# Block products with nested sums, four chained in one PSUM bank, and redrawn instruction lists for tiles 3 to 8

## The chip, the core and the metric

One NeuronCore of a Trainium2 chip runs the whole program. The metric is device time in microseconds; the runs of the kernel before gave 348.14, 348.18 and 349.24 us, a median of 348.18. Engines are named as the profile names them: PE (matrix products), PEld (its weight loads), DVE, ACT and POOL (element-wise work), SP (it only issues DMAs). POOL also issues DMAs.

## The reference

Causal attention in blocks of 64 over 8 batches, 8 heads, 576 positions and head width 64; its output, laid out as 4608 tokens by 512, goes through a gated feed-forward layer.

```python
def _attn_ref(q, k, v):
    scores = 1.0 / np.sqrt(D) * np.matmul(q, k.transpose(0, 1, 3, 2))
    scores = np.where(block_i >= block_j, scores, -1000000000.0)
    attn = np.exp(scores - np.max(scores, axis=-1, keepdims=True))
    attn = attn / (np.sum(attn, axis=-1, keepdims=True) + 1e-09)
    return np.matmul(attn, v)

def _moe_ref(x, w_gate, w_val, w_out):       # x: 4608 x 512
    gate = np.maximum(x @ w_gate, 0.0)       # 512 x 1536
    val = x @ w_val
    return gate * val @ w_out                # 1536 x 512
```

## The kernel before

**Tiles.** The feed-forward work is cut into nine tiles of 512 tokens: tile j (0 to 7) is the first 512 positions of batch j, and tile 8 collects the last 64 positions of all eight batches. Hidden values are kept transposed, in three buffers hT of four chunks (128 hidden units by 512 tokens). While tile j is in the feed-forward layer, the attention of batch j+1 is computed between its matmuls, so that tile 7 and tile 8 have no attention work beside them.

**Who sets the order.** All instructions are issued in an order written out by hand; each engine works through its own instructions in that order and waits on semaphores. Tiles 0 to 2 come from a generator of matmuls into which the other work is put at given places. Tiles 3 to 6 share one list, `ORDER_3_6`; tiles 7 and 8 have their own. A list holds tokens: `p15*2` is two steps of product 5 of pair 1 (one step is two matmuls of 128 x 256), `p1a` an element-wise step of pair 1, `g0` and `v0` one plain matmul of 128 x 512, `M4` two matmuls of out-product 4, `oa` a step of the out-projection, `A1` the score matmuls of visit 1 (one visit for two heads), `E1u` one of its exponentials, `C11` a zeroing of masked corners, `V10` the product with v of one head, `N10` its normalisation, `T2` a DMA transpose of normalised outputs on SP's queue, `l0` to `l10` the loads of q and k of the batch after next and `w0` to `w5` those of v (POOL's queue), `d0` to `d3` their DMA transposes (SP's queue), `K` the scores of the last 64 positions, `X` a sum of parts of the tile's input x, `s` a sum of parts of the hidden values, `U` a sum of weights that is made once, `S` a store.

**Seven products.** In tiles 3 to 8 the up-projection of a pair of hidden chunks (gate and value) is done as a 2 x 2 block product with seven products in place of eight. `times` (line 1331) issues one: two steps of two matmuls, left operand a weight block or a sum of weight blocks (`up_sum`, line 922), right operand a block of x or a sum of blocks (`x_sums`, line 1130). Tiles 3 to 6 take four pairs (1, 2, 3, 5) so and four chunks plainly; tiles 7 and 8 take all six pairs so. The seven products of a pair go into three PSUM tiles:

- y takes products 5, 3, 6, z takes 2, 4, 7, and m takes 1;
- ACT copies y after product 5 (`a`, line 1371) and z after product 2 (`b`, line 1374), and z again after product 4 (`l`, line 1389); a ReLU of y after product 3 gives the gate of the second half (`r`);
- DVE or POOL adds the two copies (`s`, line 1377), DVE subtracts that sum from m (`m`, line 1382), adds y (`y`, line 1393) and z (`z`, line 1396);
- the halves of the hidden pair are then `H` (a product, on POOL or DVE, line 1401) and `L` (a product with the ReLU in the same instruction, DVE, line 1415).

The out-projection (`seven_products`, line 1011) does the same with hidden sums (`Sums.make_part`, line 976, the add at line 992; 18 DVE instructions per tile) and sums of rows of w_out: products 3 and 5 in one bank, 4 and 2 in another, 1, 6 and 7 in three more; three ACT copies (`oa`, `oy`, `oz`) and six adds (line 1080).

PSUM has eight banks here: two tiles `sc` of two banks each, one tile `one`, three tiles `ffnp`. A visit needs both `sc` tiles, `one` and an `ffnp` at a time; `PAIR_BANK` says which tile takes y, z and m of each pair.

Of the kernel before, what the change touches and what calls it, by code (L numbers as in the profile page):

```python
# [17 lines left out]
def kernel(  # L18
# [23 lines left out]
    OUT_2 = (3, "oa", 4, "ob", 1, "om", 5, "oy", 2, "oz", "S0", "oc", "od", 6, "o6", "S1", 7, "o7", "S2")  # L42
# [3 lines left out]
            "010101010101010010101010101010101010101010101010101010101001110010100110"  # L46
            "100111001010011010011100101001101001110010100110100110100101"
# [3 lines left out]
            "201021102101020120120120121201202101202101202101210210201102220201101202"  # L51
            "001201202112000202112102022102102011022202011012020012012021120002021121"
            "0202210210122001201200121012012"
        ),
        "ob": (
            "043210432104310420312142324014203124304232410421302431423240142031243042"
            "324104210324103140231403"
        ),
        "gate_sb": (
            "021021021021021021021021021021021021021021011201201002102101120120100210"  # L60
            "21021021"
        ),
    }
    ORDER_3_6 = """
        A0 E0t X1 X3 X4 X6 Y4 g0 X7 E0u E0s C01 E0f g0 K g0*2 r0 k g1*2 v0*2 C00 l0 l1
        l2 v0 p15 v0 h0 p15 p1a g1*2 V00 U02 N00 r1 P V01 N01 p12*2 p1b p1s p13 l3 w0
# [4 lines left out]
        p36*2 p3y r8 p34*2 p3l V11 N11 A2 E2t E2u E2f p2L p37*2 p3z U41 w2 w3 p52*2  # L71
        s1101 p55*2 s0212 p3L p5b v8*2 V10 N10 p51 v8*2 h8 p5a p53*2 p51 p54 p5s p5m E2s
        C21 g9*2 p54 s1201 p5r p56 g9 p56 g9 p5l p57 r9 p57 v9*4 p5y p5z C20 h9 M3*2 A3
        E3t p5L s2001 E3s p3H U45 s1012 s2101 s1112 s1001 E3u p5H s2112 U05 E3f U07
        s2012 V21 N21 C31 M4 M3*2 M4 M3*2 U46 U47 w4 w5 C30 V20 N20 M1*3 M4*3 T1 T0 oa
# [4 lines left out]
        p15 p05 X1 p05 p0a p02*2 p0b p12*2 p1b p01 X3 X4 p03 p0s p03 p0r p15 p1a p04*2  # L80
        p0l p01 p1s X6 p06*2 p13*2 p1r p25*2 X7 p07*2 p0m p0y p0H Y1 p0z p0L p11 p22*2
        p11 P p2a p2b p2s p23*2 p2r p16 p14*2 p1l p16 p1m p1y p24 p26 p21*2 p26 s0101
        p24 p2l p1H p35*2 p3a p2m p2y p32*2 p27*2 p45 p3b p3s p45 p4a s0001 p2H p2z
        p17*2 p1z p33 p34 p33 p55 p42*2 p3r p34 p31*2 p2L p4b p4s p1L p3l p36*2 p55 p5a
        p3m p3y p3H s1101 p43*2 p4r p44 p37*2 p3z p3L s0112 p52 p41 p46 p52 p5b p41 p4m
        p53*2 p5r p5s p51 p44 p4l p51 p46 p4y p54 p47 p56 p54 p4H p5m p56 p5y p5l M4 p47
        p4z p57*2 p5z M3 M4 M3 M1 p5H M4*4 p4L p5L s1012 s1112 M3 s2112 s2101 M3*3 oa
        s0012 s1001 M1*5 M5 s2001 M5 s2012 M5*4 oy S0 ob M2*5 s0212 s0201 M6 s1201 s2212
        M2 M7 s1212 M6 s2201 oz S1 M6 M7 M6*3 om oc od o6 Y3 M7*4 o7 S2
    """  # L90
    ORDER_8 = """
        X6 p12*2 p1b p15*2 p1a p1s X7 p02*2 p0b p05*2 p14 p11*2 p13*2 p0a p0s p1m p01
        p03 p14 p01 p0m p03 p1r p16*2 p1y p1H p1l p17*2 p1z p0r p06*2 p04*2 P p0y p22*2
        p1L p0l p0H p2b s0112 p25*2 p32*2 p35 p07 p35 p2a p2s p07 p0z p0L p23*2 p3a p24
        p21*2 p2m p24 p2r p26*2 p3b p3s p2y p2H p55 p2l p33*2 p31 p34 p31 p34 p3r p36
        s0001 p3m p36 p3y p3H p55 p27*2 s0101 p2z p3l p37*2 p3z p52*2 p51 p5a p42 p45*2
        p5b p54 p53*2 p2L p3L p5s p42 s1001 p41 p4a p43 p41 p51 p43 p5r p56 p5m p56 p54
        p5y p4b p4s p44*2 p4m p5H p4r M3 p46*2 p5l p57 p4l p47*2 p57 M3 p4y p4z p5z M4*2
        p4H M4*3 p4L p5L M1 M4 M3*3 s1012 s1101 s2101 M3 s1112 M1 s2112 M1*3 oa s0012 M5
        s2001 M5 s2012 M5*4 ob oy S0 s2212 M2*5 M1 s0212 s2201 M2 oz S1 s1212 s0201  # L100
        s1201 M6*6 om oc o6 M7*6 S2 od o7b Sb o7a Sa
    """
    ONLY = {
        'U01': (6,),
        'U02': (6,),
# [3 lines left out]
        'U41': (6,),  # L109
        'U42': (6,),  # L110
# [3 lines left out]
        'Y4': (6,),  # L114
# [10 lines left out]
        (3, 1): ('sc', 'ffn', 'sc'),  # L125
        (3, 2): ('one', 'sc', 'ffn'),
        (3, 3): ('sc', 'ffn', 'ffn'),
        (3, 5): ('ffn', 'one', 'sc'),
        (4, 1): ('sc', 'ffn', 'sc'),
        (4, 2): ('one', 'sc', 'ffn'),  # L130
        (4, 3): ('sc', 'ffn', 'ffn'),
        (4, 5): ('ffn', 'one', 'sc'),
        (5, 1): ('sc', 'ffn', 'sc'),
        (5, 2): ('one', 'sc', 'ffn'),
        (5, 3): ('sc', 'ffn', 'ffn'),
        (5, 5): ('ffn', 'one', 'sc'),
# [33 lines left out]
    AV_BANK = {0: ('sc', 'one'), 1: ('ffn', 'ffn'), 2: ('sc', 'ffn'), 3: ('ffn', 'sc')}  # L170
    U_AT = {'U15': 300, 'U12': 306, 'U11': 312, 'U16': 386, 'U17': 389, 'U25': 320, 'U22': 326, 'U21': 332, 'U26': 392, 'U27': 395, 'U35': 340, 'U32': 346, 'U31': 352, 'U36': 398, 'U37': 401, 'U55': 360, 'U52': 366, 'U51': 372, 'U56': 404, 'U57': 407}
# [738 lines left out]

    def weight_differences(c, eng):

        two = wo[c // 2][:, 2 * (c % 2) : 2 * (c % 2) + 2, :]
        for d, n in ((two[:, 0, 256:512], two[:, 1, 256:512]), (two[:, 1, 0:256], two[:, 0, 0:256])):
            eng.tensor_tensor(out=d, in0=d, in1=n, op=AX.subtract)
# [6 lines left out]
    def up_sum(n, which):  # L922
# [6 lines left out]
        g, u = wg[i], wv[i]  # L929
        a, b, op = {  # L930
            1: (g[:, 0:2, f], u[:, 2:4, f], AX.add),
            2: (u[:, 0:2, f], u[:, 2:4, f], AX.add),
            5: (g[:, 0:2, f], g[:, 2:4, f], AX.add),
            6: (u[:, 0:2, f], g[:, 0:2, f], AX.subtract),
            7: (g[:, 2:4, f], u[:, 2:4, f], AX.subtract),
        }[which]
        if which in (6, 7):
            t = a
        else:
            where, i, k = UP_MEM[n][(5, 2, 1).index(which)]  # L940
# [11 lines left out]
    class Sums:  # L952
# [16 lines left out]
        def make(self, q, parts, k0, k1):  # L969
            while len(self.two) <= q:  # L970
                self.two.append(sb.tile([128, 2048], BF, name="stage", bufs=10))
            for part in parts:
                if part < 3:
                    self.make_part(q, part, k0, k1)
# [1100 lines left out]
```

## Time and profile before

| what | value |
|---|---|
| median of three runs | 348.18 us (348.14 to 349.24) |
| the profiled execution: its own time / its span | 348.39 us / 346.6 us |
| granted TensorE clock | 0.999 |
| instructions | 9051; 3481 matmuls recorded |
| busy PE / PEld / DVE / ACT / POOL | 334.8 / 233.9 / 273.0 / 207.5 / 194.7 us |
| read from and written to HBM | 37.75 MB and 9.44 MB |
| tile 3, 4, 5, 6 begins (score matmuls of visit 0) | 139.3, 175.3, 211.5, 247.4 us |
| tile 7, tile 8 begins (first matmul of a product) | 283.28, 312.31 us |
| last matmul ends / last DVE instruction ends | 341.72 / 342.73 us |

A busy share of an engine is the time that its instructions take in the records. Matmuls overlap: one of 128 x 256 has a duration of 273 ns, but 24 of them in a row take 2.78 us, which is (2.78 - 0.27) / 23 = 0.109 us from one start to the next, and four of 128 x 512 take 1.03 us, (1.03 - 0.38) / 3 = 0.217 us. What PE could still give away is therefore seen in the distances between starts and not in its busy share. A group of instructions names its line, its engine, the tile written and the tiles read, its count and its mean duration; the releaser behind a gap is what ended the wait.

### The profile page before, as it was taken

How to read it: one execution, taken by the hardware profiler on the slowest of the kernel's cores; microseconds unless marked ns; L12 is line 12 of the kernel's file. 1: busy time of each engine (PE TensorE's matmuls, PEld its weight loads, DVE VectorE, ACT ScalarE, POOL GpSimd, SP SyncE). 2: the span in 40 equal slices, each digit the busy share in tenths (PEclk: the TensorE clock that was granted, in tenths of full speed). 3: DMA queues.
4: the chain of work that ended last, by engine and by line, in shares of the span. 5: the costliest groups of instructions: out<-in, count | busy, mean ns of one | idle time of the engine just before them, and what ended most of it. 6: DMA issues, size and time to landing. Idle time of an engine off the chain costs nothing.

```text
span 346.6 us, 9051 instructions
## 1 busy us (share of the span) xinstructions
PE 334.8 (97%) x3481; PEld 233.9 (67%) x3518; DVE 273.0 (79%) x690; ACT 207.5 (60%) x341; POOL 194.7 (56%) x229
## 2 busy tenths in 40 slices
PE   8999999999999999999999999999999999999994
PEld 4544455545545559676977787778778788888873
DVE  4854455768629897789977997899899989999995
ACT  4942756587335872687468746884588537526721
POOL 2767566477795901986087627872155636612530
PEclk9999999999999999999999999999999999999999
DMA  8999999999999994999299929993400141012005
GB/s 244 294 352 373 360 217 242 229 155 176 184 218 113 137 191 82 190 174 139 40 158 181 152 40 156 164 171 47 121 32 2 33 129 33 2 41 83 3 0 121
DMA packets 155403, 50.07 MB, mean 144 GB/s; under 512 B 134464, under 2 KB 151744, under 8 KB 155360
## 3 DMA queue, kind: packets, MB, share of 16 engines
q1 hardware_dynamic: 77520, 32.52, 43.7%
q0 software_dynamic: 70528, 8.98, 43.3%
q10 hardware_dynamic: 7312, 8.00, 8.3%
q8 instruction: 27, 0.44, 0.5%
q14 instruction: 16, 0.13, 0.1%
HBM read 37.75 MB, written 9.44 MB: 136 GB/s over the span
## 4 chain that ended last, share of the span: by engine, by line
PE 75%; DMA 10%; DVE 9%; issue 2%; ACT 2%; POOL 1%; DVEq 0%; SPq 0%; ACTq 0%; POOLq 0%
PE ffnp L1033 11%; PE ffnp L1162 11%; PE ffnp L1348 9%; PE ffnp L1322 7%; PE sc L1348 7%; PE ffnp L1265 5%; PE one L1348 5%; PE one L1033 4%; PE sc L611 3%; DMA stage<-in_moe_w_out_dram 3%; PE ffnp L759 3%; DMA stage<-in_moe_w_val_dram 2%; DMA stage<-in_moe_w_gate_dram 2%; PE one L611 2%; DVE ob L1382 2%
## 5 line engine op out<-in xcount | busy, mean ns | idle before, releaser
L616 ACT ACTIVATE attnT<-sc 128x1024 bf16<-128x1024 f32 x56 | 56.3, 1037 | 0.0
L1033 PEld LDWEIGHTS <-stage 128*128 128x128 bf16 x420 | 39.9, 98 | 4.8 <-DVE stage L992 0.2
L992 DVE TENSOR_TENSOR stage<-hT 128x512 bf16<-128x512 bf16 (+2 forms) x120 | 39.6, 382 | 0.2
L1162 PE MATMUL ffnp<-xT,wg 128*128 128x512 bf16 x130 | 36.2, 379 | 0.6
L1172 ACT ACTIVATE gate_sb<-ffnp 128x512 bf16<-128x512 f32 x35 | 20.5, 598 | 27.0 <-PE ffnp L1162 22.7
L1080 POOL TENSOR_TENSOR ob<-ob,ob 128x512 f32<-128x512 f32 x7 | 8.9, 1268 | 45.7 <-DVE ob L1080 19.9
L1348 PEld LDWEIGHTS <-stage 128*128 128x128 bf16 x288 | 27.6, 98 | 7.4 <-issue 0.4
L759 PEld LDWEIGHTS <-attnT 128*128 128x128 bf16 x640 | 26.1, 98 | 9.2 <-DVE attnT L1526 1.1
L1033 PE MATMUL ffnp<-stage 128*128 128x256 bf16 x252 | 32.0, 273 | 0.0
L1162 PE MATMUL ffnp<-xT,wv 128*128 128x512 bf16 x108 | 31.3, 380 | 0.2
L1182 DVE TENSOR_TENSOR hT<-gate_sb,ffnp 128x512 bf16<-128x512 bf16 x28 | 19.1, 684 | 14.1 <-PE ffnp L1162 11.5
L623 ACT ACTIVATE attnT<-one 128x512 bf16<-128x512 f32 (+1 forms) x28 | 15.0, 536 | 22.2 <-PE ffnp L611 11.6
L489 POOL DMA_DIRECT2D v_bf<-in_v_dram x30 | 24.5, 826 | 3.5 <-PE sc L759 1.6
L1348 PEld LDWEIGHTS <-wg 128*128 128x128 bf16 x224 | 21.5, 98 | 5.7 <-issue 1.5
L1348 PEld LDWEIGHTS <-wv 128*128 128x128 bf16 x224 | 21.8, 98 | 4.1 <-DVE perm L1154 0.2
L1265 PE MATMUL ffnp<-wo,hT 128*128 128x512 bf16 x91 | 23.2, 379 | 0.3
L1162 PEld LDWEIGHTS <-wv 128*128 128x128 bf16 x144 | 12.9, 98 | 14.7 <-issue 1.8
L1162 PEld LDWEIGHTS <-wg 128*128 128x128 bf16 x144 | 13.4, 98 | 13.8 <-issue 0.5
L1401 POOL TENSOR_TENSOR hT<-gate_sb,ob 128x512 bf16<-128x512 bf16 x16 | 19.0, 1188 | 4.0 <-DVE ob L1393 3.9
L489 POOL DMA_DIRECT2D q_bf<-in_q_dram x20 | 18.0, 906 | 3.7 <-DVE recip L732 3.5
L611 PEld LDWEIGHTS <-kTm 64*128 64x128 bf16 x384 | 11.3, 94 | 12.9 <-issue 7.3
L1377 POOL TENSOR_TENSOR ob<-ob,ob 128x512 f32<-128x512 f32 x8 | 10.1, 1265 | 16.7 <-ACT ob L1371 10.2
(228 smaller groups left out, 911.7 us busy)
## 6 DMA issues: line engine op xcount, KB each, us to landing
out_dram<-ob ACTq DMA_DIRECT2D x28, 256.0 KB, 3.6
stage<-in_moe_w_val_dram SPq DMA_DIRECT2D x6, 512.0 KB, 8.7
stage<-in_moe_w_gate_dram SPq DMA_DIRECT2D x6, 512.0 KB, 8.3
stage<-in_moe_w_out_dram SPq DMA_DIRECT2D x6, 512.0 KB, 10.5
q_bf<-in_q_dram POOLq DMA_DIRECT2D x20, 128.0 KB, 4.8
k_bf<-in_k_dram POOLq DMA_DIRECT2D x20, 128.0 KB, 5.9
v_bf<-in_v_dram POOLq DMA_DIRECT2D x20, 128.0 KB, 6.3
stage<-in_v_dram SPq DMA_DIRECT2D x19, 128.0 KB, 5.4
```

What stands on the lines that cost most here:

```text
L489: ins = nc.gpsimd.dma_start(dst, part_of)
L611: nc.tensor.matmul(o, kTm[b % 2][head_of(hh), c, hp, :], qT, start=True, stop=True)
L616: return lambda: nc.scalar.activation(at[:, :, lo : lo + 512], sc, AF.Exp, scale=scale)
L759: nc.tensor.matmul(av[:, p, :], at[:, col : col + 128], v_bf[b % 2][:, c, h, :], start=(p == 0), stop=(c == p), skip_group_check=True,)
L992: nc.vector.tensor_tensor(out=out.rearrange("p (c n) -> p c n", c=m), in0=a, in1=b, op=op)
L1033: nc.tensor.matmul(to, sums.of(c)[which][:, 128 * p : 128 * p + 128], right, start=first, stop=(c == 5), skip_group_check=True,)
L1162: nc.tensor.matmul(to, (wg, wv)[t][f // 4][:, c, 128 * (f % 4) : 128 * (f % 4) + 128], x[:, c], start=(c == 0), stop=(c == 3),)
L1172: nc.scalar.activation(gate_sb, gate, AF.Relu)
L1182: nc.vector.tensor_tensor(out=h, in0=gate_sb, in1=val, op=AX.mult)
L1265: nc.tensor.matmul(op, hT[f][:, 128 * s : 128 * (s + 1)], wo[f // 4][:, f % 4, n0:n1], start=(f == 0), stop=(f == 11),)
L1322: nc.tensor.matmul(to, (wg, wv)[t][f // 4][:, c, 128 * (f % 4) : 128 * (f % 4) + 128], x[:, c], start=(c == 0), stop=(c == 3),)
L1348: nc.tensor.matmul(st[key][:, 256 * k : 256 * k + 256], left[:, c, 128 * k : 128 * k + 128], right[:, c], start=new and (k, c) == (0, 0), ...
```

## The change

It puts another scheme of seven products in place of the first, with sums that use each other, in both projections of tiles 3 to 8 and in the out-projection of tile 2; the same number of matmuls of the same sizes is issued (3518, 796,608 columns in all). The products of a pair now go so: the tile w takes products 1, 6, 5, 3 one after the other, v takes 7 and 4, and x takes 2. ACT copies w after product 1 (`a`) and after 6 (`u`) and v after 7 (`w`); DVE adds w after product 5 onto the copy of v (`d`), v after 4 onto the second copy (`e`) and x onto the first (`c`); `r` is the ReLU of w after product 3. `H` and `L` are as before.

- Sums of x: four in place of five, nested (5, then 6 from it, then 4 from that, and 7), three on POOL in tiles 3 to 7. Hidden sums: four parts of 512 columns for each hT buffer, 12 in place of 18 instructions, nested in the same way, five of them on POOL in tiles 3 to 7 and three in tile 8. Weight sums of the up-projection: four per pair in place of five, one written in place in wv, none in wg. Corners: five of eight on POOL.
- Out-projection: w takes products 1, 6, 5, 3 in one bank with reads `oa`, `ou` (ACT), `od` (DVE) between them and `oy` (ACT) last; v takes 7 and 4 (`ow` ACT, `oe` DVE); x takes 2 (`oc` DVE). Four ACT copies and three DVE adds.
- New lists: `ORDER_3_6`, `ORDER_7`, `ORDER_8`, `OUT_2`, `PAIR_BANK`, `OUT_BANK`, `SLOTS`, `ON_POOL`, `AV_BANK`. In `ORDER_3_6` the last loads of k (`l8`; `l9`, `l10`) and their transposes (`d1`, `d2`; `d3`) go from the first half of the list to its second half and its end. The places of the work in tiles 0 to 2 are written as a list (`ORDER_0`); up to the out-projection of tile 2 PE's instructions are the same as before.

The diff, cut:

```diff
     ORDER_3_6 = """
-        A0 E0t X1 X3 X4 X6 Y4 g0 X7 E0u E0s C01 E0f g0 K g0*2 r0 k g1*2 v0*2 C00 l0 l1
...
-        p13 p1r p11 v1*2 p11 l4 l5 p1m p14 p16*2 p1y d0 p14 p1l v1 U01 U06 U42 l6 l7 l8
-        d1 d2 A1 E1u v1 h1 p17*2 p32 E1t E1s E1f p25*2 p32 g8 p1z p1L C11 p22*2 g8*2
-        p35*2 C10 s0101 p1H s0112 p2a p23*2 p2b p24 p21 g8 p21 p24 p3b p2r p26 s0012 l9
-        l10 d3 w1 p3a p3s s0001 p26 p2s p2m p2y p2H p33*2 p31*2 p3m p2l p27*2 p2z p3r
...
-        M5 M1*2 M4 ob V31 M5 V30 M5 N31 M5*2 T2 N30 T3 M1 M5 M2*4 oy M2*2 S0 oz s0201
-        s2212 s1212 S1 s2201 M6*2 om M7 M6*3 oc od M7 M6 M7*4 o6 S2 o7
+        A0 E0u X5 X7 g0 g1*3 X6 X4 g0 p12*2 p11*2 g1 g0*2 E0f E0s p1a p1c p17*2 p16 w0
+        E0t C01 r0 K k p16 p1u C00 V00 N00 U05 l0 v1*2 p15*2 p1w p1d V01 N01 l1 l2 l3 r1
+        v0 p14*2 p1e p13*2 v0 p1L P p1r w1 l4 l5 A1 E1t E1u E1s v1*2 h1 p21 p22 p21 v0
...
+        V10 p5w p5u p54*2 p5e g9*4 p55*2 d0 E2f C20 l8 w5 N10 T1 r9 A3 E3u T0 d1 d2 v9*3
+        p5L s0102 M1 v9 p5d p53*2 E3s h9 s1102 M1*3 C21 p5r p5H E3f C30 M1 V21 s1002
+        s2102 s1202 s2002 M1 E3t V20 N21 N20 s0302 M7*2 T2 M7*3 oa M6 M7 ow C31 V31 N31
+        s2202 V30 M6 N30 M6 M4*2 M6*3 M4 U47 s2302 ou M4*3 U43 oe M5*3 T3 M5*3 od S2 S1
+        M2*6 M3 s1302 U03 M3*5 oy l9 l10 d3 oc S0
     """
     ORDER_8 = """
...
-        s1201 M6*6 om oc o6 M7*6 S2 od o7b Sb o7a Sa
...
+        p4L p5w p5d p52 p4d p54*2 p5e p5c p5L p53*2 M1 p5r p5H p43*2 p4r p4H M7 M2 M1*5
+        oa s2002 s2202 M2 oca Sa s1202 M2*3 M6*6 ou s2102 s1102 M7*2 s0302 ocb s2302
+        M7*3 ow M5*4 Sb M5*2 od s1302 S2 M4*6 M3*6 oy S0 oe S1
     """
@@ up_sum
-            1: (g[:, 0:2, f], u[:, 2:4, f], AX.add),
-            2: (u[:, 0:2, f], u[:, 2:4, f], AX.add),
-            5: (g[:, 0:2, f], g[:, 2:4, f], AX.add),
-            6: (u[:, 0:2, f], g[:, 0:2, f], AX.subtract),
-            7: (g[:, 2:4, f], u[:, 2:4, f], AX.subtract),
+            5: lambda: (u[:, lo, f], u[:, hi, f], AX.add),
+            6: lambda: (ups[n, 5], g[:, lo, f], AX.subtract),
+            3: lambda: (g[:, hi, f], ups[n, 6], AX.subtract),
+            7: lambda: (g[:, lo, f], u[:, lo, f], AX.subtract),
@@ Sums.make_part
+            even, odd = h[:, 2 * k0 : 2 * k1 : 2], h[:, 2 * k0 + 1 : 2 * k1 : 2]
+            a, b, op = {
+                0: (even[:, :, hi], odd[:, :, hi], AX.add),
+                1: (even[:, :, lo], even[:, :, hi], AX.subtract),
+                2: (of(0), even[:, :, lo], AX.subtract),
+                3: (odd[:, :, lo], of(2), AX.subtract),
+            }[part]
+            (eng or nc.vector).tensor_tensor(out=of(part), in0=a, in1=b, op=op)
@@ seven_products
+            to = {1: "w", 6: "w", 5: "w", 3: "w", 7: "v", 4: "v", 2: "x"}[which]
+            if which in (1, 7, 2):
+                st[to] = bank(OUT_BANK.get((j, to), {"w": "one"}.get(to, "ffn")))
+            yield from whole(st[to], which, which in (1, 7, 2))
...
+            if name in ("oa", "ou", "ow", "oy"):
+                key = {"oa": "c11", "ou": "c21", "ow": "c22", "oy": "c12"}[name]
+                st[key] = ob()
+                nc.scalar.copy(st[key], st["v" if name == "ow" else "w"])
+            elif name == "od":
+                add(st["c22"], st["w"])
+            elif name == "oe":
+                add(st["c21"], st["v"])
+            elif name == "oc":
+                add(st["c11"], st["x"])
@@ x_sums
+            a, b = {
+                5: lambda: (x_part(j, lo, 1), x_part(j, lo, 0)),
+                6: lambda: (x_part(j, hi, 1), shaped(xsum[j, 5])),
+                7: lambda: (x_part(j, hi, 1), x_part(j, lo, 1)),
+                4: lambda: (x_part(j, hi, 0), shaped(xsum[j, 6])),
+            }[n]()
@@ program: times, pair
-            key = n, {5: "y", 3: "y", 6: "y", 2: "z", 4: "z", 7: "z", 1: "m"}[which]
-            new = which in (5, 2, 1)
+            key = n, {1: "w_", 6: "w_", 5: "w_", 3: "w_", 7: "v_", 4: "v_", 2: "x_"}[which]
+            new = which in (1, 7, 2)
...
+            if what in "auw":
+                st[n, what] = ob({"a": "ob", "u": "k_bf", "w": "q_bf"}[what])
+                nc.scalar.copy(st[n, what], st[n, "v_" if what == "w" else "w_"])
+            elif what in "dec":
+                t, of = {"d": ("w", "w_"), "e": ("u", "v_"), "c": ("a", "x_")}[what]
+                t = st[n, t]
+                nc.vector.tensor_tensor(out=t, in0=st[n, of], in1=t, op=AX.add)
```

More of the change, by code (lines that the diff above doesn't have):

```diff
@@ L90 @@
+        M6*4 ou M7*4 ow M5*5 M4 M5 s0302 s1302 od S2 M4*5 oe M3*2 s2302 M3 S1 M3 Y7 Y6
+        oc M3*2 oy S0
     """
     ORDER_8 = """
[L92 to L96, printed above, removed]
@@ L113 @@
         'U47': (6,),
-        'Y4': (6,),
     }
@@ L957, in __init__, with room @@
             self.quads = quads
-            self.two = [sb.tile([128, 2048], BF, name="stage", bufs=10) for _ in range(3)] if j > 2 else []
-            self.one = sb.tile([128, 2048], BF, name="stage", bufs=10)
+            self.four = []
+            if j > 2:
+                self.room(2)
+        def room(self, q):
+            while len(self.four) <= q:
+                self.four.append(sb.tile([128, 2048], BF, name="stage", bufs=10))
         def step(self, f):
             if f < 8:
-                self.make(0, (f - 4,), 0, 2)
-            elif f < 11:
-                self.make(1, (f - 8,), 0, 2)
-            else:
-                self.make(2, range(3), f - 11, f - 10)
@@ L969, in make @@
[L969 to L974, printed above, removed]
[L976 to L994 removed]
+                self.make_part(0, f - 4, 0, 2)
+            elif f < 12:
+                self.make_part(1, f - 8, 0, 2)
+            else:
+                for part in range(4):
+                    self.make_part(2, part, 0, 2)
@@ L1043, in half, with whole @@
             return to[:, 256 * p : 256 * p + 256]
-        chunks = LAST_CHUNKS.get(j, tuple(range(6)))
-        def whole(to, which, new=True, cs=range(6)):
+        def whole(to, which, new):
             for p in range(2):
-                for c in cs:
-                    times(half(to, p), which, p, c, new and (p, c) == (0, cs[0]))
-                    if cs.index(c) % 2:
+                for c in range(6):
+                    times(half(to, p), which, p, c, new and (p, c) == (0, 0))
+                    if c % 2:
                         yield
@@ L1059, in products @@
         def products(which):
-            if which == 3:
-                st["y"] = psum_ffn.tile([128, 512], FP, name=slot("ffnp"), bufs=1)
-                yield from whole(st["y"], 3, cs=chunks)
-            elif which == 4:
-                st["z"] = psum_one.tile([128, 512], FP, name="one")
-                yield from whole(st["z"], 4, cs=chunks)
-            elif which in (5, 2):
-                yield from whole(st["y" if which == 5 else "z"], which, new=False)
-            elif which == 7 and j == B:
+            if which == 2 and j == B:
@@ L1069, in products @@
                 for p in range(2):
-                    st[7, p] = psum_ffn.tile([128, 512], FP, name=slot("ffnp"), bufs=1)[:, 0:256]
+                    st["x", p] = psum_ffn.tile([128, 512], FP, name=slot("ffnp"), bufs=1)[:, 0:256]
                     for c in range(6):
-                        times(st[7, p], 7, p, c, c == 0)
+                        times(st["x", p], 2, p, c, c == 0)
                         if c % 2:
                             yield
-            else:
-                st[which] = psum_ffn.tile([128, 512], FP, name=slot("ffnp"), bufs=1)
-                yield from whole(st[which], which)
@@ L1079, in add @@
[L1079 to L1105 removed]
+                return
```

645 lines of the change are left out of this document (176 added, 469 removed).

## Prediction

> **What bounds it now.** I read the page's busy times first, then the busy time by tile (windows), then the distances between PE's matmul starts in the timeline.
>
> ```profile
> PE 334.8 (97%) x3481; PEld 233.9 (67%) x3518; DVE 273.0 (79%) x690; ACT 207.5 (60%) x341; POOL 194.7 (56%) x229
> ...
> DVE  4854455768629897789977997899899989999995
> ...
> PE 75%; DMA 10%; DVE 9%; issue 2%; ACT 2%; POOL 1%; DVEq 0%; SPq 0%; ACTq 0%; POOLq 0%
> ```
>
> PE is nearly always busy and DVE is at nine tenths in the last third. The windows of tile 4, tile 7 and tile 8 (columns: length, then busy time and count of PE, PEld, DVE, ACT, POOL) say the same by tile:
>
> ```profile
> 175.30:211.50 36.20, 35.82 (x413) 27.55 (x416) 31.30 (x82) 24.12 (x40) 22.05 (x25) 1.00 1.25 135
> 283.28:312.31 29.03, 28.49 (x255) 24.27 (x253) 27.45 (x57) 14.56 (x27) 13.76 (x12) 1.00 0.12 38
> 312.31:341.72 29.41, 28.56 (x254) 24.10 (x251) 28.03 (x56) 14.99 (x27) 10.51 (x10) 1.00 0.12 33
> ```
>
> Busy PE includes overlap, so I count PE's work by pitch: 0.109 us for 128x256, 0.217 for 128x512, 0.0306 for 128x65, 0.77 for a visit's scores. Tiles 3 to 6: 112 x 0.109 + 84 x 0.109 + 32 x 0.217 + 120 x 0.0306 + 4 x 0.77, and 0.5 for K and the changes between 64 and 128 rows: 35.5 us. Their lengths are 36.0, 36.2, 35.9 and 35.8, so PE waits 1.9 us in the four. Tiles 7 and 8: 252 x 0.109 = 27.5 each, against 29.03 and 29.25 (to the next tile's start and to the last matmul): 3.2 us of waits. The matmuls stay, so **5.1 us is all that tiles 3 to 8 can give**; the other waits lie before 128 us, where PE's list is unchanged, or in tile 2's out-projection.
>
> Where the 1.9 us sits, in tile 4's timeline (start, length, instruction, idle before it and releaser):
>
> ```profile
> 180.81 0.59 ACT L1374 COPY ob<-ffnp 128x512 f32<-128x512 f32 x1 [0.38 <-PE ffnp L1348]
> 181.43 0.69 DVE L1377 TENSOR_TENSOR ob<-ob,ob 128x512 f32<-128x512 f32 x1
> 182.23 0.69 DVE L1382 TENSOR_TENSOR ob<-sc,ob 128x512 f32<-128x512 f32 x1
> 183.12 0.69 DVE L1393 TENSOR_TENSOR ob<-sc,ob 128x512 f32<-128x512 f32 x1 [0.20 <-PE ffnp L1348]
> 183.34 0.92 PE L611 MATMUL sc<-qTm,kTm 64*128 64x512 bf16 x6
> ```
>
> Visit 1 needs both `sc` tiles, which hold m and y of pair 1: a copy, `s`, `m` and `y` in a row end at 183.81, and the second half of the scores starts 0.31 to 0.44 us late, in each of the four tiles: 1.5 of the 1.9. In tiles 7 and 8 the largest waits are these two:
>
> ```profile
> 300.80 0.38 PE L1348 MATMUL ffnp<-perm,wg 128*128 128x256 bf16 x2 [0.23 <-ACT q_bf L1389]
> ```
>
> ```profile
> 331.75 0.60 PE L1033 MATMUL one<-wo,hT 128*128 128x256 bf16 x4
> 333.00 0.83 PE L1033 MATMUL one<-wo,hT 128*128 128x256 bf16 x6 [0.65 <-POOL hT L1401]
> ```
>
> In the first PE waits for the copy of z before it may add product 7 to it (0.39 between starts beyond the pitch). In the second, PE has run dry: the last `H` on POOL is the end of a long element-wise chain (0.81). Six waits of 0.17 to 0.31 make up much of the rest.
>
> **Element-wise work.** Row durations: DVE 0.69 for a f32 add with PSUM, 0.42 for 512 columns in bf16 (0.28 for 256), 0.165 for a corner; POOL 1.15 for a bf16 sum, 1.19 for `H`, 0.31 for a corner; ACT copy 0.59. Tiles 3 to 5, DVE: x sums 5 to 1 (-1.7), hidden sums 18 to 7 (-3.8), pair adds 14 to 12 (-1.4), `H` 0 to 3 (+2.1), out adds 5 to 3 (-1.4), corners 8 to 3 (-0.8): -7.0 of 35.1 by that tally (31.3 in the window, since neighbours overlap). POOL: +3 x 1.15 + 5 x 1.15 - 3 x 1.19 - 2 x 1.27 (`s`) - 1.27 (an out add) + 5 x 0.31 = +3.4 on 23.1. ACT gains a copy, +0.6. Tiles 7 and 8: DVE 30.9 to 25.0 and 24.1, which scales to 22 of the 27.5 us that PE needs; POOL 13.7 to 13.9 and 9.8 to 8.2. In no tile does any engine come near PE: DVE stops being a second bound. The sums that move to POOL hide beside PE's plain products; uncovered, one costs PE 1.15 minus what lies between.
>
> **Waits that go.** The chains to a free bank get shorter: `e` and `d` take sums that ACT copied, and there is no `s`, `m`, `y` in a row. Visit 1 then waits for one DVE add on one `sc` tile and the ReLU on the other, each already started: I put 0.1 in place of 0.37, four times (bounds 0 and 0.44). The drain in tile 8: p43 ends, `r` 0.6, `H` 0.68, two hidden sums 0.83 and hops, 2.5 to 2.9 us, beside 11 to 13 product steps of 0.218 (2.4 to 2.8): about 0 in place of 0.81 (bounds 0 and 0.8).
>
> **Waits that come.** In w the products 1, 6, 5, 3 alternate with reads, and PE may not go on before the read has ended. A link is last matmul 0.27, copy 0.59 (DVE 0.69) and hops 0.09, from the last matmul's pitch 0.84 to 0.87 by ACT, 0.94 to 0.96 by DVE. In before, ACT made every such read in mid-chain; now DVE makes the third (`d`, `od`), with its queue of adds before it; behind the waiting matmul everything on PE stands. In PE's new list the other work between the products of a bank takes 0.87 to 3.3 us; 13 links have a margin of 0.15 or less (2 in each of tiles 3 to 6, 3 in tile 7, 2 in tile 8). If the reader is just in another instruction, such a link costs about 0.55 - 0.14 = 0.41. Bounds 0 and 13 x 0.41 = 5.3. I take a quarter in tiles 3 to 6 (8 x 0.1 = 0.8) and half in 7 and 8 (5 x 0.2 = 1.0), since the row at 300.80 shows such a link late by 0.39 there, and 3 to 6 show none that large but visit 1.
>
> The Trainium skill, PSUM — Partial Sum Buffer, section "PSUM bank collisions raise a hardware error", says that two engines on the same bank and quadrant collide even in different columns, so that a guard has to be by bank: the read and the next product cannot overlap in part. The trace agrees as far as it goes (the row at 300.80 waits for the whole copy). Without that rule the 1.8 us of links would be 0, and the time 343.9.
>
> **POOL against DVE.** One pair from two views of tile 7:
>
> ```profile
> 288.21 1.27 POOL L1401 TENSOR_TENSOR hT<-gate_sb,k_bf 128x512 bf16<-128x512 bf16 x1
> ```
>
> ```profile
> 289.12 0.92 DVE L1415 SCALAR_TENSOR_TENSOR hT<-ob,q_bf 128x512 bf16<-128x512 f32 x1
> ```
>
> The DVE product takes 0.92 where others take 0.68, beside a POOL instruction; few pairs show this. Bounds for tile 7: nothing, or some 13 DVE instructions with both inputs in SBUF x 0.5 = 6.5, which makes 22 + 6.5 = 28.7, 1.2 over PE. I take 0: the product of POOL's and DVE's times of this kind falls (13.6 x 16 to 13.9 x 10.6 in tile 7). The Trainium skill, SBUF — State Buffer, section "Who interferes with whom", has it that one such DVE instruction and a GpSimd read of SBUF lock each other out for a whole instruction; by that rule the time would be up to 346.9, by the rows 345.7.
>
> **Loads and transposes.** `l9`, `l10` and `d3` go from 13 us into the tile to its end, 35.5 us; the same DMAs in number and size. POOL issues them behind the hidden sums s1302 and s2202, which wait for `H` of pair 3 and pair 5 and for one another; SP issues d3 behind T3 and the stores S1, S2. K of the next tile, 4.15 us into its list, needs kTt. In before K is earlier in its list, but kTt has 13 us to spare.
>
> ```profile
> 149.77 1.31 POOL L489 DMA_DIRECT2D k_bt<-in_k_dram  x2
> ```
>
> ```profile
> 158.78 1.21 SPq L506 DMA_TRANSPOSE kTt<-k_bt  x1
> ```
>
> kTt lands 4.4 to 5.7 after its issue, k_bt 5.9 to 6.7 (in traffic; loads of 32 KB in quiet times 2.3 to 3.4). By the dependencies l10 is issued 31.7 to 33.2 us into the tile, lands at 34 to 36.5, kTt at 38 to 41; K wants it at 40.1. Margin +2 to -1; with both at their longest, 33.2 + 6.7 + 5.7 = 45.6, it is -5.5. I take 0, since the page's slices show the DMA engines at their quietest at the tiles' ends; bounds 0 and 3 tiles x 5.5.
>
> **Tail.** From the last matmul's end (341.72) to the last store's landing 3.63 us pass:
>
> ```profile
> 339.14 0.59 ACT L1095 COPY ob<-one 128x512 f32<-128x512 f32 x1 [0.94 <-PE one L1033]
> ...
> 341.58 0.65 POOL L886 DMA_DIRECT2D out_dram<-ob  x1 [8.63 <-DVE ob L1080]
> 341.98 0.75 DVE L1080 TENSOR_TENSOR ob<-ob,ffnp 128x256 f32<-128x256 f32 x2
> ```
>
> Now a whole ACT copy (0.59, hops 0.12) ends it, then two stores on one queue (0.68 to issue the first, 2.45 to land): 3.84, +0.2 (bounds 0 and +0.5). Tile 2's new out-projection: 0 (bounds 0 and +0.4, one late link).
>
> **Sum.** Tiles 3 to 6: -1.9 + 0.4 + 0.8 = -0.7. Tiles 7 and 8: -3.2 + 1.0 + 0.2 (drain and start) = -2.0. Tail +0.2. So 348.39 - 2.5 = 345.9 for an execution like the profiled one, which lies 0.2 above the median: **345.7 us**.
>
> **Rivals.**
> 1. **All waits go.** The margins hold: -5.1 + 0.2, 343.3. For it: DVE 5 us emptier. Against: 13 thin links.
> 2. **The links eat it.** All 13 pay 0.41: -5.1 + 0.4 + 5.3 + 0.2 = +0.8, 349.0, no change. For it: the third read is on the fuller engine.
> 3. **Late keys (slower).** SP's d3 comes after T3 and the stores, with q loads of the next tile in the DMA engines; kTt lands 1.5 us after K's turn in tiles 4, 5 and 6, and all of PE stands behind K: 345.7 + 4.5 = 350.2. It decides when kTt lands over 4.15 us into the next tile. For it: 4.4 to 5.7 us of landing. Against: POOL ran 2.5 to 3 us ahead of its list in before.
> 4. **POOL blocks DVE** in tile 7, as above: 346.9.
>
> That the change does not do what it says is excluded: the counts of matmuls and columns are the same in both lists.
>
> **Chances.** Forecast 0.44, first rival 0.12, second 0.18, third 0.20, fourth 0.06. About 0.3% (347.1 to 349.2) is what a measurement of this kernel can tell from no change. Faster: 0.44 + 0.12 + 0.06, less 0.02 for the forecast's own upper end: 0.60; same 0.18 + 0.02; slower 0.20. The range goes from the first rival to the third.
>
> **What would show it.** Tiles 3 to 6 at 35.7 to 35.8 us each; visit 1's second half under 0.15 late; tiles 7 and 8 under 28.3; DVE near 25 of 36 and 22 of 28 us; PE idle behind `d` and `od` 1.8 in all; K's weight load without idle before it; last store 3.8 after the last matmul. I am wrong if K waits on the kTt transpose (third rival), or if a tile 3 to 6 grows past 36.2.

## The result, and the profile after

The changed kernel takes 351.09 us (350.91 to 351.11, four runs) against 348.23 for the kernel before: ratio 1.0074, 95% interval 1.0056 to 1.0093. It is **slower**, by 0.7%, and outside the range. The profiled execution took 350.91, with a span of 349.1.

The page of the changed kernel, the lines that answer to those shown of before:

```profile
PE 338.3 (97%) x3518; PEld 233.4 (67%) x3518; DVE 245.8 (70%) x562; ACT 211.4 (61%) x348; POOL 201.4 (58%) x248
...
DVE  4853455667538787589648973898379877986981
...
PE 76%; DMA 10%; DVE 4%; POOL 4%; ACT 3%; issue 1%; ACTq 0%; SPq 0%; POOLq 0%; DVEq 0%
```

DVE has 27 us less to do, as intended (273.0 to 245.8), and PE's share of the span has not moved. In the chain that ended last DVE went from 9% to 4%, and POOL from 1% to 4%. The windows of tile 4, tile 7 and tile 8:

```profile
175.33:212.37 37.04, 36.52 (x417) 27.50 (x418) 27.61 (x62) 24.75 (x41) 27.21 (x32) 1.00 1.37 132
286.23:315.00 28.77, 28.20 (x254) 24.30 (x252) 23.90 (x39) 15.04 (x28) 11.73 (x10) 1.00 0.11 37
315.00:343.87 28.87, 28.28 (x255) 24.38 (x252) 22.69 (x42) 15.34 (x28) 9.27 (x8) 1.00 0.16 45
```

Tiles 7 and 8 got shorter, tile 4 longer by 0.85 although its DVE fell by 3.7 us. The span splits so (us; PE's waits are the distances between matmul starts beyond the pitch and the row changes):

| stretch | before | after | difference | PE's waits before, after |
|---|---|---|---|---|
| up to the start of tile 3 | 139.31 | 138.83 | -0.48 | |
| tiles 3, 4, 5, 6 | 36.02, 36.19, 35.93, 35.83 | 36.50, 37.04, 37.28, 36.58 | +3.43 | 0.44, 0.59, 0.34, 0.36; 0.85, 1.42, 1.66, 1.04 |
| tiles 7 and 8 | 58.44 | 57.64 | -0.80 | 3.20; 2.38 |
| last matmul to the end | 4.88 | 5.23 | +0.35 | |

The first row is no result: in the experiments below, whose instructions are the same up to there, tile 3 begins at 138.9 to 139.9 (the only execution of e5 was a slow one, in which tile 3 begins at 145.3, so of that run only the lengths of the tiles are used). So the loss is new waits in tiles 3 to 6, 4.97 us in place of 1.73, which is 3.24 of the 3.43. (The gaps that missing matmul records leave in the trace of before are not counted as waits.) Three views show where. The head of tile 4, from the timeline:

```profile
175.44 0.58 ACT L1106 COPY ob<-ffnp 128x512 f32<-128x512 f32 x1 [4.22 <-PE ffnp L1061]
...
176.05 0.38 ACTq L893 DMA_DIRECT2D out_dram<-ob  x1
...
176.48 0.60 ACT L643 ACTIVATE attnT<-ffnp 128x512 bf16<-128x512 f32 x1 [0.46 <-PE sc L631]
...
178.04 0.60 PE L1354 MATMUL sc<-xT,wg 128*128 128x256 bf16 x4 [0.25 <-ACT attnT L636]
```

In before the store was issued as the visit began, and the exponentials stood right behind it, 0.44 after the visit's start (also at 175.33):

```profile
175.29 0.38 ACTq L873 DMA_DIRECT2D out_dram<-ob  x1
175.77 0.60 ACT L623 ACTIVATE attnT<-one 128x512 bf16<-128x512 f32 x1 [2.36 <-PE ffnp L611]
```

Now ACT copies the last product of the out-projection (`oy`), issues its store, and only then begins visit 0's exponentials, 1.15 us after the visit's start at 175.33. The up-projection wants an `sc` tile 2.3 us after that start (the expectation of e1 below says 1.9) and comes 0.415 too early by the distance of starts (the 0.25 in the line counts from the modelled end of the matmul before); `K` then waits 0.162 for `one`. Tiles 4, 5 and 6 do the same: 1.73 us. Tile 3 does not: its store is on SP, and its exponentials begin 0.58 after the visit's start.

Ahead of visit 3 in tile 4, from the views of POOL and of DVE, and PE at the visit:

```profile
194.48 1.63 POOL L1020 TENSOR_TENSOR stage<-hT 128x512 bf16<-128x512 bf16 x1
```

```profile
195.02 1.64 DVE L1392 TENSOR_TENSOR hT<-gate_sb,ob 128x512 bf16<-128x512 bf16 x1
```

```profile
199.54 0.39 PE L631 MATMUL sc<-qTm,kTm 64*128 64x384 bf16 x4 [0.23 <-DVE xtail L725]
```

POOL's hidden sum ran until 196.11; DVE's product `H`, which takes 0.68 alone, ended 0.55 later. The hidden sum on DVE just before it had also taken long, 1.23 in place of 0.42. Together they pushed DVE's queue, `N10` with its `xtail` in it. Visit 3 waits 0.39 for the `sc` tile that `N10` reads (0.39, 0.39, 0.39 and 0.19 in the four tiles; by e2 and e3 below the push is 0.2 of each 0.39), and g9 0.05 to 0.19 for a bank (0.42 in three tiles). In tile 5 there is a wait for POOL itself, which has the corner C11 behind loads:

```profile
227.09 0.48 PE L779 MATMUL sc<-v_bf,attnT 128*128 128x65 bf16 x10 [0.20 <-POOL attnT L1510]
```

That is 0.37 by the distance of starts. Visit 1 waits 0.18 in each tile and out-product 7 waits 0.09: 0.73 and 0.36. The sum of all is 1.73 + 1.36 + 0.42 + 0.37 + 0.73 + 0.36 = 4.97.

### The profile page after: what moved, and what is told of

Its sections match the earlier page's. It is cut to its first block, busy times and chain, and to the rows that moved or that the text cites. A ratio compares the mean times of both kernels' runs of the same rounds, so it can differ in the third digit from the quotient of the medians.

```text
span 349.1 us, 8920 instructions
## 1 busy us (share of the span) xinstructions
PE 338.3 (97%) x3518; PEld 233.4 (67%) x3518; DVE 245.8 (70%) x562; ACT 211.4 (61%) x348; POOL 201.4 (58%) x248
## 4 chain that ended last, share of the span: by engine, by line
PE 76%; DMA 10%; DVE 4%; POOL 4%; ACT 3%; issue 1%; ACTq 0%; SPq 0%; POOLq 0%; DVEq 0%
PE ffnp L1170 11%; PE ffnp L1061 10%; PE ffnp L1354 10%; PE sc L1354 7%; PE sc L1061 6%; PE ffnp L1330 6%; PE ffnp L1273 5%; PE one L1354 4%; PE sc L631 3%; DMA stage<-in_moe_w_out_dram 3%; DMA stage<-in_moe_w_val_dram 2%; DMA stage<-in_moe_w_gate_dram 2%; PE ffnp L779 2%; PE one L631 2%; PE sc L779 1%; PE one L779 1%
## 5 line engine op out<-in xcount | busy, mean ns | idle before, releaser
L1170 PE MATMUL ffnp<-xT,wg 128*128 128x512 bf16 x140 | 37.8, 379 | 0.0
L1180 ACT ACTIVATE gate_sb<-ffnp 128x512 bf16<-128x512 f32 x35 | 20.5, 599 | 26.8 <-PE ffnp L1170 26.7
L1106 ACT COPY ob<-ffnp 128x512 f32<-128x512 f32 x20 | 11.8, 590 | 39.1 <-PE ffnp L1061 34.9
L1061 PEld LDWEIGHTS <-stage 128*128 128x128 bf16 x336 | 31.6, 98 | 4.9 <-DVE stage L1020 1.2
L1170 PE MATMUL ffnp<-xT,wv 128*128 128x512 bf16 x112 | 32.0, 380 | 0.0
L1354 PEld LDWEIGHTS <-stage 128*128 128x128 bf16 x288 | 27.6, 98 | 6.5 <-issue 0.4
L1380 DVE TENSOR_TENSOR ob<-ffnp,ob 128x512 f32<-128x512 f32 x29 | 19.8, 683 | 15.0 <-ACT ob L1376 14.5
L1510 POOL MEMSET attnT<- 64x256 bf16 x22 | 7.3, 336 | 39.0 <-ACT attnT L636 19.7
L1061 PEld LDWEIGHTS <-hT 128*128 128x128 bf16 x252 | 24.2, 98 | 5.3 <-DVE hT L1396 1.2
L1325 ACT ACTIVATE gate_sb<-ffnp 128x512 bf16<-128x512 f32 x30 | 18.3, 609 | 14.9 <-PE ffnp L1354 11.1
L1354 PE MATMUL ffnp<-xT,wg 128*128 128x256 bf16 x124 | 21.1, 273 | 0.0
L1330 PE MATMUL ffnp<-xT,wv 128*128 128x512 bf16 x64 | 21.1, 380 | 0.0
```

What stands on the lines that cost most here:

```text
L1061: nc.tensor.matmul(to, sums.of(c)[which][:, 128 * p : 128 * p + 128], right, start=first, stop=(c == 5), skip_group_check=True,)
L1170: nc.tensor.matmul(to, (wg, wv)[t][f // 4][:, c, 128 * (f % 4) : 128 * (f % 4) + 128], x[:, c], start=(c == 0), stop=(c == 3),)
L1180: nc.scalar.activation(gate_sb, gate, AF.Relu)
L1325: nc.scalar.activation(st[key], of, AF.Relu)
L1330: nc.tensor.matmul(to, (wg, wv)[t][f // 4][:, c, 128 * (f % 4) : 128 * (f % 4) + 128], x[:, c], start=(c == 0), stop=(c == 3),)
L1354: nc.tensor.matmul(st[key][:, 256 * k : 256 * k + 256], left[:, c, 128 * k : 128 * k + 128], right[:, c], start=new and (k, c) == (0, 0), ...
```

## The experiments

Theory: the losses come from work on ACT, DVE and POOL that the new lists put ahead of something PE needs at once. Rivals: late keys; a full DVE; a scheme that gains nothing.

**e1_store_sp.** Store S0 of tiles 3 to 6 on SP's queue.

```diff
-            (nc.sync if j == 2 else nc.scalar).dma_start(
+            (nc.sync if j == 2 or (hi, n0) == (0, 256) else nc.scalar).dma_start(
```

> One store of each tile 3 to 6 (S0, the one behind the copy oy) is issued by SP's queue in place of ACT's. Theory: the changed kernel loses its gain at two places of tiles 3 to 6. The first is the head of tiles 4, 5 and 6: ACT copies oy, then spends 0.38 us on issuing S0, and only then begins visit 0's exponentials (1.15 us after the visit's start, 0.58 in tile 3, where the store is on SP); the up-projection wants an sc tile 1.9 us after the visit's start and waits 0.415, and K waits another 0.162 for the tile one. So here the exponentials begin 0.6 us after the visit's start, both waits go (3 x 0.58 = 1.7) and the time is 349.3 to 349.5. Rival, the x sums or the transposed x come late and hold the head: the waits stay at 0.41 and 0.16, 351.1. Rival, SP's queue delays the transposes: slower than 351.1.

349.6 us, 1.0046 of before (1.0019 to 1.0073). Timeline of its tile 4, which begins at 175.53:

```profile
176.12 0.60 ACT L643 ACTIVATE attnT<-ffnp 128x512 bf16<-128x512 f32 x1
...
177.82 0.60 PE L1354 MATMUL sc<-xT,wg 128*128 128x256 bf16 x4
```

The exponentials begin 0.59 after the visit's start, and both waits are gone in tiles 4 to 6, as expected. Tiles 3 to 6 take 146.06 (147.40 in the changed kernel), 1.34 less: most of the other 0.39 of the 1.73 comes back as a longer wait for POOL's corner (0.62 in tile 5, where it was 0.37, and 0.12 in tile 4).

**e2_sum_dve.** `3s0102`, `4s0102`, `5s0102` and `6s0102` taken out of `ON_POOL`.

> One hidden sum of tiles 3 to 6 (the second part of the first hT buffer) is done by DVE at its place in the list in place of POOL. Theory: POOL's sum runs just when DVE has the product H of pair 3 to do, both read SBUF, and DVE's product takes 1.64 in place of 0.68; the 1.0 us goes down DVE's queue to the normalisation before visit 3, whose second half waits 0.39 for an sc tile (0.19 in tile 6), and to the product h8, for which the plain chunk g9 waits 0.19. So here H takes 0.68, visit 3's wait and g9's go (1.36 + 0.42), and the time is 349.2 to 349.5, though DVE does 0.42 more. Rival, DVE's queue is simply full there and moving work onto it makes it fuller: visit 3's wait stays or grows, 351.1 to 352.5.

350.96, 1.0067 (1.0051 to 1.0083): the mechanism holds, the price does not. From its timeline:

```profile
194.37 0.68 DVE L1392 TENSOR_TENSOR hT<-gate_sb,ob 128x512 bf16<-128x512 bf16 x1
```

`H` takes 0.68 again, g9's wait is gone, but visit 3's only falls from 0.39 to 0.19 (in tile 6 it stays 0.19), product 3 of pair 5 now waits 0.12, and the corner in tile 5 0.70 in place of 0.37. Tiles 3 to 6 take 147.17, 0.23 less where 1.8 was expected. The same edit brings the hidden sum ahead of `H` from 1.23 back to 0.41, so what goes is the price of both. The 0.19 that stays is not a full queue: DVE now waits 0.40 for PE two instructions ahead of `N10`.

**e3_loads_early.** The keys.

```diff
-        V10 p5w p5u p54*2 p5e g9*4 p55*2 d0 E2f C20 l8 w5 N10 T1 r9 A3 E3u T0 d1 d2 v9*3
+        V10 p5w p5u p54*2 p5e g9*4 p55*2 d0 E2f C20 l8 l9 l10 w5 N10 T1 r9 A3 E3u T0 d1 d2 d3 v9*3
...
-        M2*6 M3 s1302 U03 M3*5 oy l9 l10 d3 oc S0
+        M2*6 M3 s1302 U03 M3*5 oy oc S0
```

> The loads l9 and l10 and the transposes d3 go back from the end of the list of tiles 3 to 6 to beside l8 and d2. Theory (the two places above): kTt lands in time as it is, since K waits only 0.16 and for another tile, so 351.1 plus or minus 0.3. The third rival of the prediction (late keys): K's wait goes and the time falls by 0.5 or more.

350.82, 1.0064 (1.0043 to 1.0085); K's 0.16 stays. In the changed kernel kTt lands 1.2 to 2.2 us before K: the keys are not late. Tiles 3 to 6 do get 0.5 shorter, for another reason: the moved loads stand ahead of POOL's sum, visit 3's wait falls to 0.18 in tiles 3 to 5, and g9's goes. In tiles 3 and 4 `H` takes 0.68 (the low product of pair 5 takes 1.12 in its place). In tile 5 `H` still takes 1.64, and only the hidden sum ahead of it is back at 0.42; visit 3 waits 0.18 there too. In tile 6 of the changed kernel it is the other way round: the hidden sum takes 1.01, `H` 0.68, and visit 3 waits 0.19. So neither of the two alone costs visit 3 anything: DVE's slack takes it up, and it needed both to push the queue.

**e4_both.** e1 and e2.

> The store on SP and the hidden sum on DVE together. Theory: the two places are apart in time and add up, -1.7 and -1.8: 347.4 to 347.8, that is 0.5 us or so below the kernel before. Rival, each only hides the other's or a third limit (ACT or DVE over the whole tile): 349 or more.

349.29, 1.0020 (1.0010 to 1.0030): the time that the rival named, and not the expected one. Tiles 3 to 6 take 145.27, 2.13 less, more than the 1.34 and 0.23 of each alone. No DVE instruction is lengthened in tiles 3 to 5. What is left per tile is 0.18 (visit 1), 0.19 (visit 3), 0.12 (product 3 of pair 5) and 0.09, and 0.37 at tile 5's corner: still more than before had. These are single waits and not a third limit over the whole tile.

**e5_corner_dve.** `C11` of tiles 3 to 6 out of `ON_POOL`, on e4.

> As e4_both, and the second corner of visit 1 (C11) is zeroed by DVE in place of POOL in tiles 3 to 6. Theory: in tile 5 the product with v waits 0.37 for POOL, which has this corner behind loads that it issues 0.4 us later in its list than in tile 4; on DVE that wait goes, tile 5 gets as long as tile 4 (36.3 from 36.6), and one execution takes about 0.4 less than e4_both. Rival, the wait is for the exponential before the corner: tile 5 stays at 36.6.

Tile 5 takes 36.34 (36.61), and its wait falls from 0.37 to 0.11, much as expected. The tiles take 145.17 together. What the edit is worth in the whole time is not shown.

**e6_order.** On e5, plain matmuls put ahead of the visits. (The chunk v9 also takes the `ffnp` bank after the next one, so that the visit keeps the next one.)

```diff
-        v0 p14*2 p1e p13*2 v0 p1L P p1r w1 l4 l5 A1 E1t E1u E1s v1*2 h1 p21 p22 p21 v0
+        v0 p14*2 p1e p13*2 v0 p1L P p1r w1 l4 l5 v1 A1 E1t E1u E1s v1 h1 p21 p22 p21 v0
...
-        ... E2f C20 l8 w5 N10 T1 r9 A3 E3u T0 d1 d2 v9*3
-        p5L s0102 M1 v9 p5d p53*2 ...
+        ... E2f C20 l8 w5 N10 T1 r9 v9 A3 E3u T0 d1 d2 v9*2
+        p5L p5d s0102 M1 v9 p53*2 ...
```

> As e5_corner_dve, with three places of the list of tiles 3 to 6 changed: one plain matmul goes ahead of visit 1, one ahead of visit 3, and the add d of pair 5 ahead of the product and the hidden sum that stood before it on DVE. Theory: what is left of waits in these tiles in e4 (0.18 at visit 1, 0.19 at visit 3, 0.12 at the fourth product of pair 5) is short and covered by one matmul of 0.22 each: 0.49 a tile or 1.9 in all, so 347.0, faster than the kernel before. Rival, the waits only move to the next reader of the same engine: 348.5 to 349.

350.16, 1.0040 (1.0025 to 1.0055): the rival. The matmul ahead of visit 3 wants a bank that ACT is still reading:

```profile
198.99 0.38 PE L1338 MATMUL ffnp<-xT,wv 128*128 128x512 bf16 x1 [0.31 <-ACT gate_sb L1329]
```

It is 0.47 late, and after visit 1 pair 2 now waits 0.10 and 0.27 for the banks of the visit that came later. Tiles 3 to 6 take 146.25, 1.1 more than in e5. The waits of visits 1 and 3 and of pair 5 are gone. Whether v9 would wait in another bank was not tried.

**e7_order_tail.** On e6, S0's stores on SP and ACT, S1's on SP and POOL.

> As e6_order, and the last two pairs of stores of tile 8 are issued by SP and ACT (S0) and by SP and POOL (S1) in place of SP twice and ACT twice. Theory: the last store lands 3.84 after the last matmul in the changed kernel because SP issues two in a row (0.65 each); issued side by side they end 0.5 earlier: e6_order less 0.5. Rival, the end is set by what follows the stores: as e6_order.

350.1, 1.0038 (1.0023 to 1.0052). S1's second store stood behind S0's on SP, so two were still issued there in a row; the last landing came 0.13 earlier after the last matmul (3.94 for 4.07), too little to be told in the time. The changed kernel has 4.07 as well, and not the 3.84 that the expectation took from the prediction.

**e8_sums_dve.** On e6, every x sum and hidden sum of tiles 3 to 6 off `ON_POOL`.

> As e6_order, with all x sums and all hidden sums of tiles 3 to 6 on DVE (DVE gets 7 to 8 sums of 0.42 more per tile, 3 us; POOL 8 us less). Theory: DVE as a whole is no bound in these tiles, single waits are; the time stays within 0.5 of e6_order, and no DVE instruction is lengthened by POOL. Rival, the change's gain is an emptier DVE: each tile gets 1 us or more longer, 351 or more.

356.69 in one execution; tiles 3 to 6 take 38.02, 38.02, 38.02 and 39.04. The rival holds. The wait is in the out-projection:

```profile
208.75 0.39 PE L1065 MATMUL ffnp<-stage 128*128 128x256 bf16 x2 [0.99 <-DVE stage L1024]
```

DVE is no bound over the tile (28.4 of 38.0 us busy in this run's tile 4) and yet its queue is one at the place where normalisations and hidden sums meet: 1.15 us there in tiles 3 to 5 and 2.11 in tile 6, and 0.41 in place of 0.09 at out-product 7. In this order, having those sums on POOL is worth more (6.8 us in the four tiles) than the change lost in all.

**e9_order2.** On e5, only the order on DVE and one product changed.

```diff
-        v0 p14*2 p1e p13*2 v0 p1L P p1r ...
+        p14*2 p1e v0 p13*2 v0 p1L P p1r ...
...
-        ... E2f C20 l8 w5 N10 T1 r9 A3 E3u T0 d1 d2 v9*3
-        p5L s0102 M1 v9 p5d p53*2 ...
+        ... E2f l8 w5 N10 C20 T1 r9 A3 E3u T0 d1 d2 v9*3
+        p5L p5d s0102 M1 v9 p53*2 ...
...
-        p4L p5w p5d p52 p4d p54*2 ...
+        p5w p5d p4L p52 p4d p54*2 ...
```

> As e5_corner_dve, with four pieces of order and no matmul put ahead of a visit: product 4 of pair 1 goes one plain matmul earlier, so that its add e frees the sc tile before visit 1; the corner C20 goes behind the normalisation N10 on DVE, so that the other sc tile is free before visit 3; the add d of pair 5 goes ahead of the low product and the hidden sum; in tile 8, d of pair 5 goes ahead of the low product of pair 4. Theory: the first three waits (0.18, 0.19, 0.12) go in each of tiles 3 to 6, which get 35.8 us each (36.3 in e5_corner_dve); in tile 8 the wait of 0.35 at product 3 goes, but DVE's burst of adds and products before the out-projection stays as long, so the later wait of 0.57 grows to 0.9 and tiles 7 and 8 together stay at 57.6. In all 346.9 to 347.3. Rival for tile 8, each link costs by itself: 57.3. Rival for tiles 3 to 6, as in e6_order the waits move on: 36.2 or more.

348.43, 0.9999 (0.9982 to 1.0017). Tiles 3 to 6 take 35.97, 35.91, 36.03 and 35.90: visit 3's wait and that of pair 5 are gone. Visit 1 keeps 0.18: the add `e` of pair 1 still stands behind the normalisation N01 on DVE, as in the changed kernel, and ends as late. Tiles 7 and 8 take 58.29, which neither side expected, and so the time misses the expected 346.9 to 347.3: product 3 of pair 4 waits 0.65, because `d` of pair 4 now stands behind the low product.

**e10_order2_tail.** On e9, `oe S1` ahead of `oy S0`; S0 on SP and ACT, S1 on POOL and SP.

> As e9_order2, and in tile 8 the add oe and its stores S1 (POOL and SP) go ahead of the copy oy, whose stores S0 are issued by SP and ACT side by side. Theory: the last store of e7_order_tail still was the second of two on SP (0.65 each); with one on each queue it lands 3.4 to 3.5 after the last matmul in place of 3.8, and the time is 0.35 below e9_order2. Rival, the landings of four stores at once take longer and the end stays: as e9_order2.

348.1, 0.9979 (0.9960 to 0.9999). The last store lands 3.65 after the last matmul, 4.07 in e9: 0.42 earlier, though not the expected 3.4 to 3.5.

**e11_best.** On e10, tile 8's piece as in the changed kernel.

> As e10_order2_tail, with tile 8's order as in the changed kernel again (low product of pair 4, then d of pair 5, then d of pair 4). Theory: in e9_order2 and e10_order2_tail the add d of pair 4 stood behind that low product, product 3 of pair 4 waited 0.65 for it, and tiles 7 and 8 took 58.29 in place of 57.65; so here 57.65 again and 0.64 less in all: 347.4 to 347.6, some 0.8 below the kernel before. Rival, the 0.64 came from the list elsewhere: 348.1.

347.39, 0.9950 of before (0.9925 to 0.9975; the medians, 347.39 and 348.60, give 0.9965): **faster than both kernels**, by half a per cent or less. Tiles 3 to 6 take 144.05, just what they took before (143.97); tiles 7 and 8 take 57.65 in place of 58.44.

**e12_d_first.** On e10, `p5w p5d p52 p4d p4L`.

> As e10_order2_tail, with both adds d (pair 5, pair 4) ahead of the low product of pair 4 in tile 8. Theory: the two links are no longer late (0.35 at product 3 of pair 5 in the changed kernel, 0.65 at that of pair 4 in e9_order2), but DVE has the same adds and products to do before the out-projection can go on, so the wait for the low product of pair 5 grows by as much, and tiles 7 and 8 stay at 57.5 to 57.7. Rival, each link costs by itself: 57.3 or less.

348.55, 0.9989 (0.9970 to 1.0008), with tiles 7 and 8 at 58.81: worse than both expectations. From its timeline:

```profile
330.20 1.16 POOL L1020 TENSOR_TENSOR stage<-hT 128x512 bf16<-128x512 bf16 x1
...
330.60 1.30 DVE L1396 SCALAR_TENSOR_TENSOR hT<-ob,k_bf 128x512 bf16<-128x512 f32 x1
...
332.56 0.38 PE L1061 MATMUL one<-wo,stage 128*128 128x256 bf16 x2 [1.17 <-DVE k_bf L1380]
```

The low product came beside a POOL sum and took 1.30 in place of 0.68; the add that frees `one` was behind it, and PE waited 1.33. Here the lock, in which one of the two engines stands until the other is done, is on PE's path, and its 0.62 is in the 1.33.

## Why the prediction was wrong

- **"Tiles 3 to 6: -1.9 + 0.4 + 0.8 = -0.7."** This is the step that failed: +3.43, with all four tiles past the 36.2 that I had named as the sign of being wrong. (Before had 1.73 of waits there by the distances of starts, not 1.9, and visit 1 had 1.35 of them, not 1.5.) I priced the waits that before shows and those inside the chains of products, and no wait at the places where the new list puts two streams against each other. At the tile's head I counted the moved loads of POOL and SP, but not the copy `oy` and the store that ACT now does ahead of visit 0's exponentials, nor that the up-projection wants an `sc` tile there so soon. e1 shows it: 1.73 of waits gone by moving one store. The other places are visit 3 and g9 (1.36 and 0.42; e2 takes 0.6 and 0.42 of them, and the rest goes in e9, where the corner C20 no longer stands ahead of `N10`) and POOL's corner (0.37; e5). With these pieces tiles 3 to 6 are back at 143.82 in e9, so the places account for the whole loss.
- **"I take 0"** for POOL against DVE. The product of busy times falls, as I said, but the lock is no matter of averages: the one POOL sum that falls on `H` costs DVE 0.96 at once. I had bounded it for tile 7 alone; it struck in tiles 3 to 5 on the way to a visit. With the sum before it, it cost PE 0.2 at visit 3 and up to 0.19 at g9; to move the POOL sum gave back 0.23 by itself (e2) and 0.79 on top of e1 (146.06 to 145.27 in e4). In e12 it cost DVE 0.62. In tile 7, where I looked, three DVE instructions are lengthened (by 0.11, 0.96 and 0.95), and PE has no wait within 5 us behind any of them.
- **"To POOL"**: corners moved at no cost, I said, by counting only their length. C11 stands behind loads: 0.37 in tile 5, 0.11 in e5.
- **Waits that go.** Visit 1's wait fell from 0.31 to 0.44 a tile to 0.18 (I took 0.1): right in kind. The drain of tile 8 fell from 0.81 to 0.57, not to 0: DVE's adds, low products and `H` stand there in a row.
- **Tiles 7 and 8: -2.0** came out at -0.80. The links I feared cost less: two are late, product 3 of pair 4 in tile 7 (0.26) and product 3 of pair 5 in tile 8 (0.35). Most of the rest are waits for DVE's burst ahead of the out-projection, 0.38 for `one`, 0.42 and 0.57 for a low product:

```profile
304.90 0.60 PE L1061 MATMUL one<-wo,hT 128*128 128x256 bf16 x4 [0.22 <-DVE k_bf L1380]
...
306.73 0.50 PE L1061 MATMUL ffnp<-wo,hT 128*128 128x256 bf16 x3 [0.26 <-DVE hT L1396]
```

DVE is busy 23.9 of 28.8 us in tile 7, and in a row when PE needs it.
- **The links.** Forecast 1.8; in the changed kernel the two late ones cost 0.61, both in tiles 7 and 8. In tiles 3 to 6 a late link shows only once the other waits are gone, 0.12 a tile (e4). But the price of a link is what DVE has before the add: 0.35 or 0.65 by the place of one low product in tile 8 (e9).
- **Loads and transposes: 0.** Right. kTt landed 39.9 us into tile 3, inside the 38 to 41 worked out, and K came at 41.1. (K came 0.6 later there than PE's work alone would bring it; in e11, without the waits at the head, kTt is still 1.0 to 2.3 us ahead of K.) The slower side came out, but not by the third rival.
- **Tail: +0.2** was +0.35, by two stores in a row on SP, the mechanism worked out; the last one lands at 4.07 in place of 3.84. e10 takes most of it back.

That DVE was relieved was right (27 us). What the new scheme is worth in the best order tried shows in e11 against before: nothing in tiles 3 to 6, 0.8 in tiles 7 and 8. How much of that is DVE's relief was not separated. Some 0.4 us of waits per tile was all that tiles 3 to 6 had to give.

## What to carry to other kernels

Here PE's waits were already down to 0.4 us in a tile of 36: a lighter DVE had next to nothing to give, and each reordering was a chance to lose. In such a kernel, look at each place where the new order wants a bank soon after a visit, a copy or a store, and write down what stands ahead of its last reader on that reader's queue, DMA issues included. Price an engine's relief by the waits that end on it, not by its busy time. Undo parts one at a time: one store moved to another queue gave back 1.34 of the 3.43 us lost in tiles 3 to 6.

## What was not expected of the hardware

In these runs a DVE instruction that reads two tiles from SBUF and a POOL instruction that reads SBUF exclude each other, whichever comes first: `H` 1.64 in place of 0.68 and ended 0.55 after POOL's sum; POOL's sum itself 1.63 in place of 1.16 behind DVE's low product. DVE's adds with one input in PSUM kept 0.68 beside a POOL sum (333.62 in the changed kernel). Beside POOL's memsets DVE's sums kept 0.42 to 0.43 (six cases in the out-projections of tiles 3 to 5), and beside its DMA issues 0.41 to 0.43. The Trainium skill, SBUF — State Buffer, section "Who interferes with whom", says just this: two SBUF inputs on DVE contend with a GpSimd instruction that reads SBUF, not with one that only writes it, and the lock on the shared ports is exclusive. The rows above agree, and the prediction gave that rule too little.

One thing stays open: in tiles 3 to 5 of the changed kernel another sum on DVE took 1.24 in place of 0.42 beside POOL's loads, just ahead of POOL's own sum; with that sum gone from POOL (e2) it took 0.41. `H` in tile 5 of e3 is such a case too: its 1.64 us ran from 232.27 to 233.91, beside loads that POOL issued, while POOL's sum began only at 233.70. Whether the sum already waiting on POOL did it was not tried.
